# Exponents and phases of the S4D responses in two 64-row halves of the matmul array

## The chip, the cores and the metric

The kernel runs on one core of one Trainium2 chip. A core has a matrix engine (TensorE: PE for its matmuls, PEld for its weight loads), a vector engine (VectorE: DVE), an activation engine (ScalarE: ACT), a general engine (GpSimd: POOL) and a queue engine (SyncE: SP). They work side by side and wait for each other by semaphores. The metric is device time in microseconds; the time before is the median of three runs, 559.39 us (557.99 to 559.58).

## What is computed

Two branches over an input u of 2048 positions and 640 channels are mixed by a gate. The first is a convolution with a response K that is made from 128 states per channel; the second is a filter in the two-dimensional frequency plane.

```python
def _A_ref(u, log_A_real, A_imag, C_real, C_imag, log_dt, D_skip):
    dt = jnp.exp(log_dt)
    A = -jnp.exp(log_A_real) + 1j * A_imag
    C = (C_real + 1j * C_imag) * dt[:, None]
    P = jnp.exp((A * dt[:, None])[:, :, None] * pos[None, None, :])
    K = 2.0 * jnp.einsum("dn,dnl->dl", C, P).real          # 640 x 2048
    ...                                                    # y = causal convolution of u with K, by rfft / irfft
    return y + u * D_skip[None, None, :]

def _B_ref(x, w_r, w_i):
    return irfft2(rfft2(x) * (w_r + 1j * w_i))

g = sigmoid((x * gate_w).sum(-1, keepdims=True))
return g * _A_ref(...) + (1 - g) * _B_ref(...)
```

The change touches how K is made, nothing else.

## The kernel before

The body has three stages. In the first, `phase_p` prepares the parameters of the responses and `phase_a` begins the transform of u along the positions. In the second, two streams are merged: `ga` goes on with `phase_a` (the rest of the transform, the frequency filter and its way back; lines L372 to L640) and `phase_c` (the first transform of K), and `gl` runs `phase_b`, which makes K. In the third, `phase_d` multiplies the transforms of u and K, goes back and mixes.

`merge` issues the two streams in turn: each yields a weight for what it has issued, and the stream that has done the smaller share of its total (164.29 for `ga`, 76.8 for `gl`, the sum of its yields) goes next. The order so written is a priority; the tile framework's planner then fixes an order for each engine at compile time and may let later work pass earlier work that it expects to be waiting. On the chip each engine works through its own list in order.

`phase_b` works on 40 groups of 16 channels, with the 128 states on the partitions. A position is written as an outer step (64 j, 32 values) plus an inner one (64 values, symmetric about 31.5). For each group t:

- `mags(t)`: an exponent for 64 inner and 32 outer positions of 16 channels, 1536 columns. The rates lie in 96 rows (6 for each channel: three bf16 parts of the rate, three of the log magnitude of C), and a table `rm` that is zero outside each channel's own rows spreads them. Three matmuls (L700) of 96 rows and 512 columns go to one bank of PSUM each, and an Exp (L702) follows each. Five groups are done in a row, since Exp and Sin use different tables of ACT.
- `phases(t)`: outer phases (columns 512 to 1023) and inner phases (0 to 511) in revolutions. Each takes three accumulating matmuls (L710) over 128 rows: the phase plus a large constant, minus that constant (which rounds it), minus the phase. What is left is the negative of the fraction of a revolution.
- `trig(t)`: for the outer phases Abs (L723), Sin (L724) and a second Sin of the absolute value with a quarter turn as bias (the cosine, L725) on ACT, into `sc` in SBUF. For the inner phases the absolute value is taken on DVE (L720, a bitwise and), and ACT makes the sine `sx` (L726) and cosine `cx` (L727) into two PSUM banks of their own (pool `pt`, one buffer each).
- `prods(t)`: DVE multiplies the exponentials by sx (L734, L735) and cx (L736) to `x`; POOL multiplies the outer ones by sc (L739, L740) to `y`. It is issued after the phases and sines of group t+1.
- `kgen(t)`: 64 small matmuls of 32 weight columns (L753), four side by side in four column groups of the array, sum over the states; an ACT copy (L759) for each two groups and a store for each ten.

PSUM has 8 banks; in this stage `ga` has 3, the pool `ps` of p_e and p_p has 2 buffers of one bank, `pk` has 1 and `pt` has 2. The parameters of five groups come by two DMAs that POOL issues in `load` (L690).

The tile names in the profile are those of the code: p_e and p_p are the PSUM tiles of exponents and phases, e the exponentials, aq the absolute values. A tile written `128*64` is the part of the array that a matmul uses: rows by columns.

Of the kernel before, what the change touches and what calls it, by code (L numbers as in the profile page):

```python
# [9 lines left out]
F32 = mybir.dt.float32  # L10
BF = mybir.dt.bfloat16
I32 = mybir.dt.int32
# [8 lines left out]
N = 128  # L21
# [28 lines left out]
def _tables():  # L50
# [67 lines left out]


    j = np.arange(32)  # L120
    rp = np.zeros((4, 32, 2, 16, 32))
    rn = np.zeros((4, 32, 512))
    rn[0, 24] = -MAGIC
    one_row = np.zeros((8, 4, 8, 5, N))
    one_row[:, :, 0] = 1.0
    rm = np.zeros((16, 6, 16, 96))
    for x in range(16):
        g, i = x // 4, 6 * (x % 4)
        rp[g, i:i + 3, 0, x] = j + 0.5
        rp[g, i:i + 3, 1, x] = 64 * j  # L130
        rp[g, i + 3:i + 6, 1, x] = 1.0
        rm[x, 0:3, x, 0:64] = A_ORDER
        rm[x, 0:3, x, 64:96] = 64 * j
        rm[x, 3:6, x, 64:96] = 1.0
    rp, rn = rp.reshape(128, 1024), rn.reshape(128, 512)
    rq = rp.copy().reshape(4, 32, 2, 16, 32)
    for x in range(16):
        rq[(x // 4 + 2) % 4, 24, :, x] = MAGIC
    rp = np.concatenate([rq.reshape(128, 1024), -rp, rn], 1)
    f = lambda x: np.ascontiguousarray(x, dtype=np.float32)  # L140
    h = lambda x: np.ascontiguousarray(x, dtype=mybir.dt.np(BF))
    return {"t_c1": f(c1), "t_w2": f(w2), "t_w3": f(w3), "t_td": f(td),
            "t_rp": h(rp), "t_one": h(one_row), "t_rm": h(rm.reshape(96, 1536))}


def _lay_out(u, log_a, a_i, c_r, c_i, log_dt, d_skip, w_r, w_i, gate_w):
# [49 lines left out]
def body(tc, A, out):  # L196
    nc = tc.nc
    T = Ctx()
    with ExitStack() as top:
# [25 lines left out]
        with ExitStack() as cctx:  # L225
            def left():
                with ExitStack() as ctx:
                    T.bc = ctx.enter_context(tc.tile_pool(name="b_c", reuse_waits="tile", bufs=1))
                    T.rm = T.bc.tile([96, 1536], BF, name="rm")
                    T.rp = T.bc.tile([128, 2560], BF, name="rp")  # L230
                    yield from phase_p(tc, A, T)
                    yield from phase_b(tc, A, T, ctx)

            ga, gl = chain(phase_a(tc, A, T), phase_c(tc, A, T, cctx)), left()
            next(gl)
            next(ga)
            for n in (6, 15):
                next(gl)
                while len(T.cps) < n:
                    next(ga)  # L240
            next(gl)
            while T.pin is None:
                next(ga)
            merge((164.29, ga), (76.8, gl))
            phase_d(tc, A, T, cctx, out)


# [417 lines left out]
def phase_b(tc, A, T, ctx):  # L665
# [20 lines left out]

    def load(b0):
        for k in (1, 0):
            par = w2.tile([128 - 32 * k, BT, N], BF, tag="par%d" % k, name="par%d" % k)
            G.dma_start(par[:, :, :], par_v[k][b0 // BT])  # L690
            for t in range(b0, b0 + BT):
                pars[k][t] = par[:, t - b0, :]

    def mags(t):
        e = es[t] = ep.tile([128, 16, 96], F32, tag="e", name="e")
        ef = e.rearrange("p d i -> p (d i)")
        for c in range(0, 1536, 512):
            p = ps.tile([128, 512], F32, tag="ps", name="p_e")
            with after(T.pin):
                P.matmul(p[:, :], pars[1][t], rm[:, c:c + 512], start=True, stop=True)  # L700
            with after(st.trig):
                st.exp = S.activation(ef[:, c:c + 512], p[:, :], AF.Exp)  # L702
            yield 0.2

    def phases(t, r):
        r.p = {}
        for c in (512, 0):
            p = r.p[c] = ps.tile([128, 512], F32, tag="ps", name="p_p")
            for i, w in enumerate((rp[:, c:c + 512], rn, rq[:, c:c + 512])):
                P.matmul(p[:, :], pars[0][t], w, start=i == 0, stop=i == 2)  # L710
            yield 0.22

    def trig(t, r):

        aq = wt.tile([128, 2, 16, 32], F32, tag="w", name="aq")
        sc = r.sc = wt.tile([128, 2, 16, 32], F32, tag="w", name="sc")
        sx, cx = r.sx, r.cx = [pt.tile([128, 16, 32], F32, tag=n, name=n) for n in ("sx", "cx")]
        fl = lambda t: t.rearrange("p d i -> p (d i)")
        af = aq.rearrange("p v d i -> p (v d i)")
        V.tensor_scalar(out=af[:, 0:512].bitcast(I32), in0=r.p[0][:, :].bitcast(I32), scalar1=0x7FFFFFFF, scalar2=None, op0=ALU.bitwise_and)  # L720

        with after(st.exp):
            S.activation(af[:, 512:1024], r.p[512][:, :], AF.Abs)  # L723
        S.activation(fl(sc[:, 0]), r.p[512][:, :], AF.Sin, scale=TWO_PI)  # L724
        S.activation(fl(sc[:, 1]), af[:, 512:1024], AF.Sin, scale=-TWO_PI, bias=T.hpi)  # L725
        S.activation(fl(sx), r.p[0][:, :], AF.Sin, scale=TWO_PI)  # L726
        T.trig = st.trig = S.activation(fl(cx), af[:, 0:512], AF.Sin, scale=-TWO_PI, bias=T.hpi)  # L727

    def prods(t, r):
        e, sx, cx, sc = es[t], r.sx, r.cx, r.sc  # L730
# [32 lines left out]
    def run():  # L763
        pend = []
        load(0)
        yield 0.0
        for t in range(40):
            if t % BT == 0:
                if t:
                    prods(t - 1, rs[t - 1])  # L770
                    pend.append(t - 1)
                for x in range(t, t + BT):
                    yield from mags(x)
                    if len(pend) > 1:
# [12 lines left out]
        for x in (*pend, 39):  # L787
            yield from kgen(x)
# [268 lines left out]
```

## Time and profile before

| | |
|---|---|
| median of three runs | 559.39 us (557.99 to 559.58) |
| the profiled execution's own time | 560.56 us |
| its span, first to last instruction | 558.8 us |
| granted TensorE clock | 0.984 |
| PE / DVE / ACT / POOL busy, share of the span | 92% / 80% / 61% / 49% |

The profile has a page (busy times, slices, a chain of waits that ended last, the costliest groups of instructions) and views that can be asked: groups by line, one tile's instructions, waits, a timeline, and busy times in given windows. In a row of a group, the figures after the bar are the union of its busy time in us and the mean ns of one instruction, then the idle time of its engine just before them and who ended most of it. Matmuls are pipelined: the duration of one includes the way through the array, so that three in a row take much less than three times one. What a matmul costs in a stream is read from the starts in the timeline. Some matmul records are missing: 212 of the 240 phase matmuls are there.

### The profile page before, as it was taken

What the parts mean: (1) busy time and instruction counts of PE and PEld (TensorE: products, weight loads), DVE (VectorE), ACT (ScalarE), POOL (GpSimd) and SP (SyncE); (2) the same over time, 40 slices, a digit from 0 to 9 for tenths busy, and PEclk for the clock granted to TensorE, in tenths of its full rate; (3) what the DMA queues carried; (4) which work ended last, traced back from release to release, by engine and by line L of the source; (5) the groups of instructions that cost most, each with busy time, mean ns of one, the idle gap of its engine ahead of it and who ended that gap; (6) DMA issues with size and microseconds to landing.
All of it is one profiled execution on the core that took longest, in us unless ns stands there. A gap on an engine that the chain in (4) does not pass through costs nothing.

```text
span 558.8 us, 16697 instructions
## 1 busy us (share of the span) xinstructions
PE 516.2 (92%) x7124; PEld 394.9 (71%) x7152; DVE 447.5 (80%) x684; ACT 339.8 (61%) x626; POOL 273.9 (49%) x277
## 2 busy tenths in 40 slices
PE   8899899997989899998999989999799999999975
PEld 6789456665857576867777766767787887787741
DVE  5997279479799979999979979876296885977945
ACT  4674677585587689797899786898224223241210
POOL 4993254056246327346257546165163446648433
PEclk9999999999899999999999999999899999999979
DMA  8969233165250331353222132115958989899877
GB/s 322 373 203 347 95 111 110 21 234 187 64 197 17 129 123 60 81 166 128 79 60 71 49 81 95 54 49 190 390 210 267 347 285 354 281 294 316 259 237 265
DMA packets 47697, 100.61 MB, mean 180 GB/s; under 512 B 3492, under 2 KB 32952, under 8 KB 45960
## 3 DMA queue, kind: packets, MB, share of 16 engines
q1 hardware_dynamic: 25176, 67.41, 34.7%
q10 hardware_dynamic: 20080, 22.52, 12.4%
q0 software_dynamic: 2368, 9.64, 5.1%
q8 instruction: 56, 0.92, 0.7%
q14 instruction: 17, 0.14, 0.1%
HBM read 60.22 MB, written 39.65 MB: 179 GB/s over the span
## 4 chain that ended last, share of the span: by engine, by line
PE 37%; DVE 6%; DMA 3%; ACT 3%; issue 1%; ACTq 0%; DVEq 0%; POOL 0%; SPq 0%
PE p_s L372 6%; PE p_s L385 6%; PE p_i L893 5%; PE p_e L172 3%; PE p_p L710 2%; PE p_k L753 2%; PE p_c L972 2%; DMA s_d<-s 2%; PE p_e L700 2%; PE p_i L633 2%; PE p_t L557 2%; PE p_eo L618 2%; PE p_eo L619 1%; PE p_d L573 1%; PE p_d L574 1%
## 5 line engine op out<-in xcount | busy, mean ns | idle before, releaser
L385 PE MATMUL p_s<-t,w 128*64 128x160 f32 x1056 | 90.5, 308 | 4.7 <-ACT ut L420 2.3
L385 PEld LDWEIGHTS p_s<-t,w 128*64 128x64 f32 x1056 | 75.4, 136 | 15.3 <-issue 4.3
L739 POOL TENSOR_TENSOR y<-e,sc 128x512 f32<-128x512 f32 x40 | 53.5, 1339 | 57.3 <-ACT sc L724 42.6
L702 ACT ACTIVATE e<-p_e 128x512 f32<-128x512 f32 x120 | 69.2, 608 | 14.0 <-PE p_e L700 12.7
L710 PE MATMUL p_p<-rp,par 128*128 128x512 bf16 x212 | 63.0, 380 | 8.1 <-ACT sx L726 4.5
L373 ACT COPY t<-p_s 128x512 f32<-128x512 f32 x40 | 24.8, 623 | 63.6 <-PE p_s L372 46.8
L753 PEld LDWEIGHTS p_k<-x,y 128*32 128x32 f32 x2560 | 42.2, 109 | 25.1 <-issue 20.7
L753 PE MATMUL p_k<-x,y 128*32 128x64 f32 x2560 | 55.5, 222 | 0.9 <-DVE x L735 0.8
L740 POOL TENSOR_TENSOR y<-e,sc 128x512 f32<-128x512 f32 x40 | 53.7, 1342 | 0.0
L700 PE MATMUL p_e<-rm,par 96*128 96x512 bf16 x120 | 43.4, 383 | 7.6 <-ACT e L702 4.3
L862 DVE TENSOR_TENSOR ma<-p_s,us 128x640 f32<-128x640 f32 (+1 forms) x36 | 28.2, 783 | 27.7 <-issue 22.0
L736 DVE TENSOR_TENSOR x<-e,cx 128x1024 f32<-128x1024 f32 x40 | 48.4, 1209 | 0.0
L372 PEld LDWEIGHTS p_s<-c,kt 128*64 128x64 f32 x640 | 39.2, 139 | 12.6 <-issue 7.1
L372 PE MATMUL p_s<-c,kt 128*64 128x128 f32 x640 | 44.6, 278 | 3.4 <-issue 2.2
L893 PE MATMUL p_i<-t,w 128*64 128x160 f32 x528 | 43.6, 306 | 3.9 <-POOL t L868 3.6
L895 ACT COPY s<-p_i 128x640 f32<-128x640 f32 x32 | 21.7, 694 | 38.7 <-PE p_i L893 23.4
L868 POOL TENSOR_TENSOR t<-mb 64x320 f32<-64x320 f32 (+1 forms) x36 | 29.9, 832 | 30.5 <-DVE t L868 30.1
L893 PEld LDWEIGHTS p_i<-t,w 128*64 128x64 f32 x528 | 37.4, 139 | 8.8 <-POOL t L868 4.3
L868 POOL TENSOR_TENSOR t<-ma 64x320 f32<-64x320 f32 x32 | 28.3, 886 | 29.9 <-DVE ma L862 28.7
L372 PE MATMUL p_s<-c,u 128*64 128x128 f32 x640 | 40.3, 276 | 0.8 <-ACT ut L420 0.6
L372 PEld LDWEIGHTS p_s<-c,u 128*64 128x64 f32 x640 | 35.3, 136 | 7.4 <-issue 5.3
L710 PEld LDWEIGHTS <-par 128*128 128x128 bf16 x240 | 21.3, 97 | 25.9 <-issue 12.0
(164 smaller groups left out, 1172.6 us busy)
## 6 DMA issues: line engine op xcount, KB each, us to landing
u_d<-ut SPq DMA_DIRECT2D x32, 320.0 KB, 2.8
us<-u_d ACTq DMA_DIRECT2D x16, 640.0 KB, 6.2
s_d<-s ACTq DMA_DIRECT2D x15, 640.0 KB, 9.2
t<-s_d SPq DMA_DIRECT2D x14, 640.0 KB, 6.8
ww<-in_w_l SPq DMA_DIRECT2D x8, 642.0 KB, 5.1
ue<-u_d SPq DMA_DIRECT2D x8, 640.0 KB, 4.2
k_d<-kt SPq DMA_DIRECT2D x4, 1280.0 KB, 4.5
kt<-k_d SPq DMA_DIRECT2D x8, 640.0 KB, 5.6
```

What stands on the lines that cost most here:

```text
L372: nc.tensor.matmul(p[64 * ri:64 * ri + 64, j, :], src(i + j), e1[ri], start=True, stop=True)
L385: ins = nc.tensor.matmul(p[64 * j:64 * j + 64, i, 160 * ri:160 * ri + 160], w2[:, x, 64 * ri:64 * ri + 64], t1[:, x // 2 if x < 32 else K0 ...
L700: P.matmul(p[:, :], pars[1][t], rm[:, c:c + 512], start=True, stop=True)
L702: st.exp = S.activation(ef[:, c:c + 512], p[:, :], AF.Exp)
L710: P.matmul(p[:, :], pars[0][t], w, start=i == 0, stop=i == 2)
L736: V.tensor_tensor(out=x[:, 0].rearrange("p d (h j) -> p d h j", h=2), in0=e[:, :, 0:64].rearrange("p d (h j) -> p d h j", h=2), in1=cx.uns ...
L739: G.tensor_tensor(out=y[:, 1], in0=e[:, :, 64:96], in1=sc[:, 0], op=ALU.mult)
L740: G.tensor_tensor(out=y[:, 0], in0=e[:, :, 64:96], in1=sc[:, 1], op=ALU.mult)
L753: P.matmul(st.pb[32 * r:32 * r + 32, o, :], y[:, ri, 4 * qq + JR[r], :], x[:, ri, 4 * qq + JR[r], :], start=t % 2 + qq + 1 - ri == 0, stop ...
L862: V.tensor_tensor(out=ma[:nl, :hn], in0=pv, in1=uu, op=ALU.mult)
L868: return eng.tensor_tensor(out=t2[64 * im:64 * im + 64, o, :], in0=m[l, :hn, 0, :], in1=m[l, :hn, 1, :], op=ALU.add if im else ALU.subtract)
L893: T.mm = P.matmul(p[x:x + 64, i // 2, 160 * (i % 2):160 * (i % 2) + 160], T.w3[:, k0 + h + i, x:x + 64], t2[:, h + i, :], start=True, stop ...
```

## The change

The tables `rm` and `rp` are laid out in two halves of 64 rows, and 8 of the 16 channels of a group lie in each. The array is used as two parts of 64 rows and 128 columns, each with its own bank of PSUM: a matmul pair in place of one.

- Exponents: 1536 columns for 16 channels become 768 for 8 channels in each half, as a pair of 512 columns and a pair of 256 (48 rows of each half are used). The two Exps are over 1024 and 512 elements in place of three over 512. The parameter block of the exponents goes to partitions 0 to 47 and 64 to 111 by two DMAs in place of one.
- Outer phases: three accumulating pairs of 256 columns. Abs and both Sins read the two banks as one operand of 2 x 256.
- Inner phases: the cosine gets columns of its own, with a quarter of a revolution taken off in the table, so that half the columns give the sine and half the cosine. Three accumulating pairs of 512 columns; one Sin over 1024 elements, written back in place in PSUM. The bitwise and on DVE and the Sin with a bias go.
- The pool `ps` has two buffers of two banks in place of one bank; `pt` goes. `prods` reads the inner sines where the phases were, in a buffer of `ps`.
- `prods(t-1)` is now issued between the outer and the inner phases of t. The yields of `phase_b` change, and the total of `gl` with them (63.76).

```diff
-            merge((164.29, ga), (76.8, gl))
+            merge((164.29, ga), (63.76, gl))
...
-    wt = ctx.enter_context(tc.tile_pool(name="b_w", reuse_waits="tile", bufs=5))
+    wt = ctx.enter_context(tc.tile_pool(name="b_w", reuse_waits="tile", bufs=3))
+    wa = ctx.enter_context(tc.tile_pool(name="b_a", reuse_waits="tile", bufs=2))
...
-    pt = ctx.enter_context(tc.tile_pool(name="b_pt", reuse_waits="tile", bufs=1, space=PSUM))
...
-    rp, rq, rn = rp[:, 0:1024], rp[:, 1024:2048], rp[:, 2048:2560]
+    steps = rp[:, 0:768], rp[:, 768:1280], rp[:, 1280:2048]
...
         for k in (1, 0):
-            par = w2.tile([128 - 32 * k, BT, N], BF, tag="par%d" % k, name="par%d" % k)
-            G.dma_start(par[:, :, :], par_v[k][b0 // BT])
+            par = w2.tile([128, BT, N], BF, tag="par%d" % k, name="par%d" % k)
+            if k:
+                for j in range(2):
+                    G.dma_start(par[64 * j:64 * j + 48], par_v[1][b0 // BT, 48 * j:48 * j + 48])
+            else:
+                G.dma_start(par[:, :, :], par_v[0][b0 // BT])
...
     def mags(t):
-        ef = e.rearrange("p d i -> p (d i)")
-        for c in range(0, 1536, 512):
-            p = ps.tile([128, 512], F32, tag="ps", name="p_e")
+        ef = e.rearrange("p (j d) i -> p j (d i)", j=2)
+        for c, n in ((0, 512), (512, 256)):
+            p = ps.tile([128, 2, 512], F32, tag="ps", name="p_e")
             with after(T.pin):
-                P.matmul(p[:, :], pars[1][t], rm[:, c:c + 512], start=True, stop=True)
+                for j in range(2):
+                    x = slice(64 * j, 64 * j + 48)
+                    P.matmul(p[:, j, 0:n], pars[1][t][x], rm[x, c:c + n], start=True, stop=True)
             with after(st.trig):
-                st.exp = S.activation(ef[:, c:c + 512], p[:, :], AF.Exp)
-            yield 0.2
+                st.exp = S.activation(ef[:, :, c:c + n], p[:, :, 0:n], AF.Exp)
+            yield n * 0.0005
...
+    def phases(t, c, n):
+        p = ps.tile([128, 2, 512], F32, tag="ps", name="p_p")
+        for i, w in enumerate(steps):
+            y = 0 if i == 1 else c
+            for j in range(2):
+                x = slice(64 * j, 64 * j + 64)
+                P.matmul(p[:, j, 0:n], pars[0][t][x], w[x, y:y + n], start=i == 0, stop=i == 2)
+        return p
+
+    def outer(t, r):
+        p = phases(t, 512, 256)
+        aq = wa.tile([128, 2, 256], F32, tag="a", name="aq")
         sc = r.sc = wt.tile([128, 2, 16, 32], F32, tag="w", name="sc")
+        sv = sc.rearrange("p v (j d) i -> p v j (d i)", j=2)
         with after(st.exp):
+            S.activation(aq[:, :, :], p[:, :, 0:256], AF.Abs)
+        S.activation(sv[:, 0], p[:, :, 0:256], AF.Sin, scale=TWO_PI)
+        S.activation(sv[:, 1], aq[:, :, :], AF.Sin, scale=-TWO_PI, bias=T.hpi)
+
+    def inner(t, r):
+        p = phases(t, 0, 512)
+        f = p.rearrange("p j w -> p (j w)")
+        T.trig = st.trig = S.activation(f, f, AF.Sin, scale=TWO_PI)
+        r.sx, r.cx = f.rearrange("p (d v i) -> p v d i", v=2, i=32)[:, 0], f.rearrange("p (d v i) -> p v d i", v=2, i=32)[:, 1]
...
             rs[t] = Ctx()
-            yield from phases(t, rs[t])
-            trig(t, rs[t])
+            outer(t, rs[t])
+            yield 0.11
             if t % BT:
                 prods(t - 1, rs[t - 1])
                 pend.append(t - 1)
+            inner(t, rs[t])
+            yield 0.22
             if len(pend) > 2:
                 yield from kgen(pend.pop(0))
```

More of the change, by code (lines that the diff above doesn't have):

```diff
@@ L120, in _tables @@
     j = np.arange(32)
-    rp = np.zeros((4, 32, 2, 16, 32))
-    rn = np.zeros((4, 32, 512))
-    rn[0, 24] = -MAGIC
     one_row = np.zeros((8, 4, 8, 5, N))
     one_row[:, :, 0] = 1.0
-    rm = np.zeros((16, 6, 16, 96))
-    for x in range(16):
+    rm = np.zeros((2, 64, 8, 96))
+    rp = np.zeros((2, 32, 8, 96))
+    for x in range(8):
         g, i = x // 4, 6 * (x % 4)
[L129 to L139, printed above, removed]
+        rp[g, i:i + 3, x, 0:32] = rp[g, i:i + 3, x, 32:64] = j + 0.5
+        rp[g, i:i + 3, x, 64:96] = 64 * j
+        rp[g, i + 3:i + 6, x, 64:96] = 1.0
+        rp[g, 24, x, 32:64] = -0.25
+        rm[:, 6 * x:6 * x + 3, x, 0:64] = A_ORDER
+        rm[:, 6 * x:6 * x + 3, x, 64:96] = 64 * j
+        rm[:, 6 * x + 3:6 * x + 6, x, 64:96] = 1.0
+    rq = rp.copy()
+    for x in range(8):
+        rq[1 - x // 4, 24, x] = MAGIC
+    flat = lambda v: np.concatenate([v[..., 0:64].reshape(64, 512), v[..., 64:96].reshape(64, 256)], 1)
+    rn = np.zeros((64, 512))
+    rn[24] = -MAGIC
+    rp = np.tile(np.concatenate([flat(rq), rn, flat(-rp)], 1), (2, 1))
     f = lambda x: np.ascontiguousarray(x, dtype=np.float32)
@@ L228, in left @@
                     T.bc = ctx.enter_context(tc.tile_pool(name="b_c", reuse_waits="tile", bufs=1))
-                    T.rm = T.bc.tile([96, 1536], BF, name="rm")
-                    T.rp = T.bc.tile([128, 2560], BF, name="rp")
+                    T.rm = T.bc.tile([128, 768], BF, name="rm")
+                    T.rp = T.bc.tile([128, 2048], BF, name="rp")
                     yield from phase_p(tc, A, T)
@@ L701, in mags @@
             with after(st.trig):
-                st.exp = S.activation(ef[:, c:c + 512], p[:, :], AF.Exp)
-            yield 0.2
[L705 to L715, printed above, removed]
+                st.exp = S.activation(ef[:, :, c:c + n], p[:, :, 0:n], AF.Exp)
@@ L716, in trig @@
         sc = r.sc = wt.tile([128, 2, 16, 32], F32, tag="w", name="sc")
[L717 to L720, printed above, removed]
+        sv = sc.rearrange("p v (j d) i -> p v j (d i)", j=2)
         with after(st.exp):
-            S.activation(af[:, 512:1024], r.p[512][:, :], AF.Abs)
```

6 lines of the change are left out of this document (1 added, 5 removed).

## The prediction

> **What bounds the kernel now.** First the busy times of the three stages, to see where the change can act at all.
>
> ```profile
> core 0: us, PE busy (x) PEld busy (x) DVE busy (x) ACT busy (x) POOL busy (x), PEclk, DMA share, GB/s
> 0.00:66.00 66.00, 59.00 (x991) 50.64 (x991) 49.58 (x62) 39.46 (x76) 40.30 (x37) 1.00 0.79 280
> 66.00:396.00 330.00, 311.21 (x4402) 227.60 (x4427) 278.45 (x423) 258.75 (x484) 153.03 (x146) 0.99 0.32 107
> 396.00:558.80 162.80, 145.97 (x1736) 116.66 (x1735) 119.43 (x199) 41.63 (x68) 80.59 (x94) 0.96 0.84 289
> ```
>
> The merged stage is 330 us long, and PE (311), DVE (278) and ACT (259) are all near its length. POOL and the DMAs have room. Which of the three sets the pace is read from the chain that ended last, here between 272 and 376 us (it reaches no further back), with the pieces of one place in it.
>
> ```profile
> by line: PE p_p L710 12.3%; PE p_e L700 9.6%; PE p_i L633 9.4%; PE p_t L557 8.6%; PE p_eo L618 8.3%; PE p_k L753 8.0%; PE p_eo L619 7.6%; PE p_d L573 5.2%; PE p_d L574 4.9%; ACT cx L727 1.8%; ACT sc L725 1.8%; DVE mm L594 1.8%; DVE ff L606
> ...
> 331.34 0.60 DVE aq L720
> 331.94 0.61 DVE x L735
> 332.57 0.59 ACT sx L726
> 333.20 0.81 PE p_p L710 x3
> ...
> 342.44 0.69 DVE aq L720
> ```
>
> The nine PE entries make 73.9%: most of this chain is PE going from one matmul to the next. The two groups that the change rewrites, L710 and L700, are 21.9% of 104 us, 22.8 us. The first four pieces show the other kind of place: ACT's Sin waits until DVE has read the one buffer of sx, and PE waits for that Sin.
>
> **Matmul time.** What a matmul costs in a stream is read from starts.
>
> ```profile
> 208.14 0.44 PE L574 MATMUL p_d<-td,ft 65*128 65x160 f32 x2
> 208.41 0.44 PE L573 MATMUL p_d<-td,ft 128*128 128x161 f32 x2
> 208.69 0.81 PE L710 MATMUL p_p<-rp,par 128*128 128x512 bf16 x3
> 209.33 0.44 PE L574 MATMUL p_d<-td,ft 65*128 65x161 f32 x2
> ...
> 415.59 1.31 PE L893 MATMUL p_i<-t,w 128*64 128x160 f32 x16
> 416.67 0.77 PE L172 MATMUL p_e<-t3e,c 128*64 128x320 f32 x4
> ```
>
> Three phase matmuls take 209.33 - 208.69 = 0.64 us, 0.215 each. A group t has nine such matmuls (six L710, three L700): 1.935 us. No row shows two halves of rows side by side. The nearest is halves of columns: 16 matmuls of 64 columns in 416.67 - 415.59 = 1.08 us, 0.135 for a pair, as much as one of the full width (0.27 for the two of 208.14). If pairs of row halves do the same, a pair of 512 costs 0.215 and one of 256 half of it, 0.1075. After the change a group has four of 512 (one in the exponents, three inner) and four of 256: 1.29 us. That saves 0.645, times 40 25.8 us. The chain had 22.8 us of these lines where 104/330 of 40 groups, 12.6, cost 12.6 x 1.935 = 24.4: 93% is on the path. I take **-24.0**. With no overlap at all it is +24.0. I take the end with overlap, by the column rows, which are the nearest.
>
> The weight loads go from 9 to 16 a group. They stay hidden by the row of the column halves, where each recorded load is as long as the pair that covers it and two are needed.
>
> ```profile
> L385 PEld LDWEIGHTS p_s<-t,w 128*64 128x64 f32 x1056 | 75.4, 136 | 15.3 <-issue 4.3
> ```
>
> **Changing the shape of the array.** A matmul that uses another split of the array than the one before it starts late.
>
> ```profile
> 368.87 0.82 PE L710 MATMUL p_p<-rp,par 128*128 128x512 bf16 x3
> 369.62 0.46 PE L557 MATMUL p_t<-c,ff 64*128 64x64 f32 x4
> ...
> 360.35 0.38 PE L700 MATMUL p_e<-rm,par 96*128 96x512 bf16 x1
> 360.57 0.44 PE L618 MATMUL p_eo<-td,pmt 128*128 128x161 f32 x2
> ...
> L710 PE MATMUL p_p<-rp,par x212: 376/379/390, 70.6 to 381.4; 128*128 128x512 bf16 x106
> ...
> L700 PE MATMUL p_e<-rm,par x120: 376/379/634, 57.6 to 364.6; 96*128 96x512 bf16 x120
> ```
>
> From p_p in the full array to a tile of 64 rows it is 0.75 us for three, 0.10 over 0.645; from p_e (96 rows, the full array) to p_eo it is 0.22, nothing over 0.215. So today's exponents and phases slip between the full-width work of the other stream for free, and the 64-row pairs will pay on each side. I counted the neighbours in PE's timeline from the first of them to the last (57.6 to 381.4): the matmuls of the two lines lie in 171 unbroken runs, and 208 of their 342 sides, 61%, border on full-width work; the others border on p_k or other narrow tiles and pay already. After the change there are 160 tiles of pairs; with the 256-column exponents often next to another pair I take 130 runs: 260 x 0.61 x 0.10 = 15.9 us, 93% on the path, **+14.8**. Bounds: 80 new changes (runs twice as long) +8, all 320 sides +30.
>
> The Trainium skill has this as a rule against such a change: "Mode switching requires drain" (TensorEngine Tiling (Array Packing), Key Properties). The trace agrees, with 0.10 us at each change; by the rule alone no sum can be made.
>
> **DVE and ACT.** The rows of what goes and of what is merged:
>
> ```profile
> L702 ACT ACTIVATE e<-p_e 128x512 f32<-128x512 f32 x120 | 69.2, 608 | 14.0 <-PE p_e L700 12.7 <-POOL fg L541 0.2
> L895 ACT COPY s<-p_i 128x640 f32<-128x640 f32 x32 | 21.7, 694 | 38.7 <-PE p_i L893 23.4 <-DMA s_d<-s 9.3 <-DVE mb L863 5.5
> ...
> L634 ACT COPY s<-p_i 128x320 f32<-128x320 f32 x34 | 14.5, 441 | 4.4 <-PE p_i L633 4.4
> ...
> L726 ACT ACTIVATE sx<-p_p 128x512 f32<-128x512 f32 x40 | 23.9, 597 | 16.4 <-DVE x L735 15.6 <-DVE aq L720 0.5
> L727 ACT ACTIVATE cx<-aq,c 128x512 f32<-128x512 f32 x40 | 27.9, 698 | 1.8 <-DVE x L736 1.8
> L720 DVE TENSOR_SCALAR aq<-p_p 128x512 int32<-128x512 int32 x40 | 27.3, 683 | 8.2 <-PE p_p L710 7.6 <-issue 0.5
> ```
>
> DVE loses 40 x 683 ns = 27.3 us. On the chain of 104 us L720 has the two pieces quoted above, 1.29 together; times 330/104 = 3.17 that is **-4.1**. Bounds: 0, and -27.3 if DVE set the pace all the way. ACT: the copies of 640 and 320 elements give (694 - 441)/320 = 0.79 ns an element, so an instruction of 1024 costs 608 + 512 x 0.79 = 1012 as an Exp and 597 + 405 = 1002 as a Sin. Three Exps (1824) become 1620, and sx with cx (1295) becomes 1002: 0.50 us a group, 20 us of ACT's 259. On the chain stands cx with 1.8% of 104, 5.9 us over the stage; merging takes 293 of its 698 ns: **-2.5**, bounds 0 and -6 (cx gone).
>
> **The buffers.** In place of four banks there are two buffers of two. The inner sines stay where the phases were until `prods` has read them: one of two buffers is blocked through Sin (1.0 us) and three products on DVE.
>
> ```profile
> L736 DVE TENSOR_TENSOR x<-e,cx 128x1024 f32<-128x1024 f32 x40 | 48.4, 1209 | 0.0
> ...
> ACT sx L726 <- DVE x L735: 15.6, 10, 3.0
> ```
>
> Today DVE's delay stops ACT: ten times, 15.6 us, and 1.8 more before cx. Afterwards that wait falls to PE: the outer pair of t+2 needs the buffer that `prods(t)` frees, and behind it in PE's list stand the matmuls of the other stream, whose copies ACT and DVE then miss. It is also released later, by L736 and not by L735, 1.21 us. From below the cost is 0 (the planner lets other matmuls pass); from above all 17.4 us fall to PE and each of the ten gets 1.21 longer: +29.5. The one place where the chain shows this coupling is quoted above, and there it costs 1.21 more and saves the Sin's 0.59; at one in 104 us that is 0.62 x 3.17 = 2, and I take **+3.0**, near the lower end, since PE has other work ready through most of the stage.
>
> **What costs nothing.** POOL issues 8 more parameter DMAs:
>
> ```profile
> L690 POOL DMA_DIRECT2D par<-par_d x12 | 6.8, 570 | 31.7 <-PE p_g L459 16.6 <-PE p_e L700 9.8 <-PE p_p L710 3.8
> ```
>
> 8 x 0.57 = 4.6 us of a POOL that is busy 153 of 330; the products L739 wait behind them, and if they were late each time it would be 4.6. The bytes are the same. The smaller tables load before 57.6, when nothing waits for them. Three buffers for sc and two for aq replace five shared ones, and each user waits for what it waited for. The new weights of `merge` move the streams against each other with the same end; bounds unknown in sign, a few us either way in the range.
>
> **Sum.** -24.0 + 14.8 - 4.1 - 2.5 + 3.0 = -12.8 us. The span goes from 558.8 to 546.0, the profiled execution's own 560.56 to 547.8; the median of the runs lies 1.17 below that execution, so **546.6**. Its own range is 540 to 553.
>
> **Rivals.**
> - *Slower: PE takes over ACT's wait.* The buffer mechanism at its upper end, +29.5 in place of +3.0: 573.1. It decides from the point where the wait costs more than 15.8 us. For it: ACT's 17.4 us of waits, and DVE at 278 of 330. Against: in the 104 us of chain the coupling shows once.
> - *The pairs don't overlap, or only in part.* With none, +24.0 in place of -24.0: 594.6. With half, 570.6. For it: no row shows row halves together. Against: column halves do.
> - *No gain: PE loses on changes of shape what it saves.* All 320 sides at 0.10, +30 in place of +14.8: 561.8. Or a pair costs 1.3 of one matmul, a third of the way to no overlap: 1.29 x 1.3 = 1.68 a group, 0.258 saved, 9.6 us on the path in place of 24.0: 561.0. For it: 0.10 stands in the rows; against the second, the column halves.
> - *DVE sets more of the pace.* If the bitwise and counts for 12 us and not 4.1, as it would where DVE is busiest, 538.7. For it: DVE's 278 us; against, the chain.
>
> The Trainium skill gives a speedup of 3.07 for four row tiles side by side (TensorE: Matmul & The Clock Gate, Measured speedup vs the span model), not 4; a pair that lost the same share would cost 1.30 of one matmul, the second form of the last-but-one rival. No run here shows row tiles yet.
>
> **How the numbers follow.** Forecast 0.46; DVE sets more 0.14; no gain 0.14; PE's wait 0.17; little or no overlap 0.09. A measurement of this kernel tells 0.3%, 1.7 us, from no change. Faster by more: 0.46 + 0.14 + 0.02 of the no-gain case = 0.62; within: 0.10 of it; slower: 0.02 + 0.17 + 0.09 = 0.28. The range from 533 to 574 takes in all but the worst overlap and the tails.
>
> **What would show it.** The two matmuls of a pair of p_p start a few ns apart, and the next pair 0.215 us later: the overlap. 0.10 us at each side of a run: the changes of shape. No bitwise and, and DVE near 251 us in the stage; ACT near 239. Idle time of PE before p_p that ends with DVE's x L736: the buffers. The forecast is wrong if PE waits there for more than 15 us, or if pairs start 0.2 us apart.

## The result, and the profile after

The changed kernel took 585.23 us, the median of four runs (583.25 to 587.75); the kernel before took 559.49 beside it. The ratio is 1.046, 95% interval 1.040 to 1.051: slower by 26 us, where 13 us faster had been forecast. Here and below, medians and ratios leave out the slow runs, those more than 1.5% above the fastest of the same kernel. The profiled execution took 584.63 us, its span is 582.8, the granted clock 0.968 (before 0.984).

The busy times of the three stages, with the columns of the first fence of the prediction:

```profile
0.00:66.00 66.00, 59.65 (x1002) 51.76 (x1002) 49.43 (x62) 39.77 (x73) 41.38 (x39) 0.97 0.76 276
66.00:420.00 354.00, 316.91 (x4692) 226.50 (x4686) 266.35 (x383) 248.98 (x406) 147.10 (x152) 0.96 0.31 100
420.00:583.00 163.00, 145.23 (x1750) 116.36 (x1746) 118.39 (x199) 42.29 (x68) 80.77 (x94) 0.98 0.84 286
```

All of the loss lies in the merged stage: 354 us for 330, the others as before. In it PE is busy for 316.9 us (311.2 before) and idle for 37.1 (18.8 before), and its clock is 0.96 for 0.99. So of 24.0 us, 18.3 are new idle time of PE and 5.7 more busy time, although it streams less. DVE (278.5 to 266.4) and ACT (258.8 to 249.0) have less to do, and still the stage is longer.

First the two things that were meant. PE's timeline of the changed kernel (start, duration to the modelled end, engine, line, operation, tiles, count):

```profile
207.88 0.50 PE L718 MATMUL p_p<-rp,par 64*128 64x256 bf16 x6
208.31 0.54 PE L575 MATMUL p_d<-td,ft 65*128 65x161 f32 x2
...
209.78 0.44 PE L574 MATMUL p_d<-td,ft 128*128 128x161 f32 x2
210.15 0.82 PE L718 MATMUL p_p<-rp,par 64*128 64x512 bf16 x6
210.91 0.54 PE L575 MATMUL p_d<-td,ft 65*128 65x161 f32 x2
211.28 0.44 PE L574 MATMUL p_d<-td,ft 128*128 128x160 f32 x2
211.56 0.43 PE L575 MATMUL p_d<-td,ft 65*128 65x160 f32 x2
```

Six phase matmuls of 64 rows and 512 columns hold PE for 210.91 - 210.15 = 0.76 us: three times 0.215, plus 0.10 for the change of shape behind them. Before, three full ones took 0.64. So the two halves of a pair run side by side, fully. Six of 256 columns take 0.43, which is half of 0.64 plus 0.10. And the two f32 matmuls ahead of a run take 0.37 where two take 0.27 in a stream: 0.10 on that side as well. There is a third 0.10, which neither the forecast nor its count of sides has: the two f32 matmuls behind the run take 211.28 - 210.91 = 0.37 too, and only the next two the usual 211.56 - 211.28 = 0.28.

Next what PE waited for in the merged stage, from the view of waits of each kernel (who <- for whom: us in total, times, longest). Before:

```profile
PE p_p L710 <- ACT sx L726: 4.5, 5, 1.4
PE p_e L700 <- ACT e L702: 4.3, 5, 1.4
PE p_p L710 <- ACT sc L724: 2.1, 4, 1.1
```

After:

```profile
PE p_e L707 <- DVE x L744: 11.1, 4, 4.4
PE p_p L718 <- ACT sc L728: 6.4, 16, 0.7
PE p_i L634 <- DVE xx L584: 4.4, 2, 2.3
PE p_s L386 <- DVE ut L421: 4.0, 2, 3.0
PE p_s L373 <- POOL kt L823: 3.2, 1, 3.2
PE p_p L718 <- DVE x L744: 2.0, 6, 0.6
```

L744 is the last of the products of `prods` (L736 before): it lets go of the two banks in which the inner sines lie. PE waits 13.1 us for it, most of it not before the phases but before the *exponents*, and four times only; the longest is 4.4. The waits behind it (xx, ut, kt) belong to the other stream; that they follow from its late turn is not shown.

The longest of these waits, on DVE and PE:

```profile
175.30 0.82 DVE L599 TENSOR_TENSOR pm<-zz 128x642 f32<-128x642 f32 x1
176.04 0.82 DVE L600 TENSOR_TENSOR pm<-zz 128x642 f32<-128x642 f32 x1
176.78 0.68 DVE L743 TENSOR_TENSOR x<-e,p_p 128x512 f32<-128x512 f32 x1
177.38 1.65 DVE L606 TENSOR_TENSOR ff<-pm 128x640 f32<-128x640 f32 x1
178.95 1.88 DVE L607 TENSOR_TENSOR ff<-pm 128x640 f32<-128x640 f32 x1
180.75 1.21 DVE L744 TENSOR_TENSOR x<-e,p_p 128x1024 f32<-128x1024 f32 x1
...
177.21 0.44 PE L575 MATMUL p_d<-td,ft 65*128 65x161 f32 x2
182.01 0.61 PE L707 MATMUL p_e<-rm,par 48*128 48x512 bf16 x2 [4.37 <-DVE x L744]
182.55 0.90 PE L574 MATMUL p_d<-td,ft 128*128 128x160 f32 x2
183.25 0.74 PE L575 MATMUL p_d<-td,ft 65*128 65x160 f32 x2
```

And the busy times in this place, with the columns of the first fence:

```profile
172.00:177.00 5.00, 4.62 (x71) 3.63 (x66) 5.00 (x10) 3.02 (x6) 0.68 (x2) 1.00 0.79 239
177.00:182.00 5.00, 0.64 (x5) 0.49 (x4) 5.00 (x5) 1.71 (x2) 4.68 (x5) 0.77 0.16 60
179.00:180.00 1.00, 0.00 (x0) 0.00 (x0) 1.00 (x2) 0.00 (x0) 1.00 (x1) 0.87 0.06 10
182.00:184.00 2.00, 1.99 (x10) 1.22 (x13) 2.00 (x5) 1.02 (x1) 0.00 (x0) 0.50 0.00 0
184.00:188.00 4.00, 4.00 (x66) 3.46 (x67) 1.97 (x4) 0.60 (x1) 1.06 (x2) 0.68 0.00 0
186.00:186.50 0.50, 0.50 (x3) 0.50 (x3) 0.00 (x0) 0.00 (x0) 0.44 (x2) 0.50 0.00 0
186.50:187.00 0.50, 0.50 (x4) 0.39 (x3) 0.00 (x0) 0.00 (x0) 0.20 (x1) 0.93 0.00 0
```

DVE is never idle here. Between two products of the same group stand two operations of the filter, L606 and L607, and they take 1.65 and 1.88 us, twice their usual 0.82 (as pm has it), while POOL is busy for 4.68 of these 5 us. PE's list has the exponents next, they need the banks that L744 reads, and the ready matmuls of p_d stand behind them. The price isn't over when the wait is: the granted clock is 0.50 in the next two us and 0.68 in the four after that, and two f32 matmuls behind a run take 183.25 - 182.55 = 0.70 us for the 0.37 above. The Trainium skill says that the array's clock falls to half after an idle window of about 3.4 us (TensorE: Matmul & The Clock Gate, Part 1). The rows agree on the half, but not on the time: PE's last matmul ended at 177.65 (a modelled end), and the clock fell between 179 and 180 (0.87 in that us, 0.50 later), after some 2 us. By 187 it was full again (0.50 from 186.0 to 186.5, 0.93 from 186.5 to 187.0).

### The profile page after: what moved, and what is told of

Read it like the earlier page. It is cut to its first block, busy times and chain, and to the rows that moved or that the text cites. A ratio compares the mean times of both kernels' runs of the same rounds, so it can differ in the third digit from the quotient of the medians.

```text
span 582.8 us, 17178 instructions
## 1 busy us (share of the span) xinstructions
PE 521.8 (90%) x7432; PEld 394.6 (68%) x7432; DVE 434.2 (74%) x644; ACT 331.0 (57%) x546; POOL 269.2 (46%) x285
## 3 DMA queue, kind: packets, MB, share of 16 engines
q10 hardware_dynamic: 20080, 22.52, 11.9%
## 5 line engine op out<-in xcount | busy, mean ns | idle before, releaser
L709 ACT ACTIVATE e<-p_e 128x1024 f32<-128x1024 f32 x80 | 62.5, 812 | 32.3 <-PE p_e L707 28.7
L747 POOL TENSOR_TENSOR y<-e,sc 128x512 f32<-128x512 f32 x40 | 52.1, 1303 | 39.7 <-ACT sc L728 22.9
L718 PE MATMUL p_p<-rp,par 64*128 64x256 bf16 (+1 forms) x480 | 52.8, 327 | 9.7 <-ACT sc L728 6.4
L761 PEld LDWEIGHTS p_k<-x,y 128*32 128x32 f32 x2560 | 44.2, 115 | 20.5 <-issue 19.3
L761 PE MATMUL p_k<-x,y 128*32 128x64 f32 x2560 | 56.8, 229 | 0.1
L744 DVE TENSOR_TENSOR x<-e,p_p 128x1024 f32<-128x1024 f32 x40 | 48.5, 1212 | 0.0
L734 ACT ACTIVATE p_p<-p_p 128x1024 f32<-128x1024 f32 x40 | 41.0, 1024 | 9.2 <-ACT sc L729 4.9
L707 PE MATMUL p_e<-rm,par 48*128 48x512 bf16 (+1 forms) x160 | 30.5, 346 | 14.6 <-DVE x L744 11.1
L742 DVE SCALAR_TENSOR_TENSOR x<-e,p_p 128x512 f32<-128x512 f32 x40 | 27.2, 681 | 21.5 <-ACT p_p L734 19.9
```

Source lines behind the costliest of these rows:

```text
L707: P.matmul(p[:, j, 0:n], pars[1][t][x], rm[x, c:c + n], start=True, stop=True)
L709: st.exp = S.activation(ef[:, :, c:c + n], p[:, :, 0:n], AF.Exp)
L718: P.matmul(p[:, j, 0:n], pars[0][t][x], w[x, y:y + n], start=i == 0, stop=i == 2)
L734: T.trig = st.trig = S.activation(f, f, AF.Sin, scale=TWO_PI)
L744: V.tensor_tensor(out=x[:, 0].rearrange("p d (h j) -> p d h j", h=2), in0=e[:, :, 0:64].rearrange("p d (h j) -> p d h j", h=2), in1=cx.uns ...
L747: G.tensor_tensor(out=y[:, 1], in0=e[:, :, 64:96], in1=sc[:, 0], op=ALU.mult)
```

## The experiments

At the start three theories were open. **A**: the loss is that of banks held until DVE has done its products. **B**: it lies in PE's own work or in the order in which the two streams are issued. **C**: it is POOL's parameter loads. Each comparison below is with the kernel before, run on the same chip.

**e1, the sines to SBUF.** The changed kernel, with the inner Sin written to SBUF, so that ACT frees the banks.

```diff
-        f = p.rearrange("p j w -> p (j w)")
-        T.trig = st.trig = S.activation(f, f, AF.Sin, scale=TWO_PI)
+        f = wa.tile([128, 1024], F32, tag="s", name="sx")
+        T.trig = st.trig = S.activation(f[:, :], p.rearrange("p j w -> p (j w)"), AF.Sin, scale=TWO_PI)
```

> The changed kernel, with one edit: the inner Sin writes to a tile in SBUF (two buffers) and not in place in PSUM, so that a buffer of phases comes free when ACT has read it and not when DVE has made its products. Theory A (PE waits for the buffer that DVE's products hold): PE's idle time before the exponents and phases that ends with DVE's x L744 (11.1 us in 4 waits and 2.0 us in 6) is gone, the low clock behind the long waits with it, and the time falls from 585 to 560-570 us. Rival B (the changes of shape of the array alone make it slow): it stays at 580-588. Rival C (POOL's parameter loads, late): it stays too.

Measured: 617.24 us, ratio 1.101 (1.096 to 1.106). PE no longer waits for L744, as A wants, but the kernel is slower still, where 560 to 570 had been expected. The products of the changed kernel, and then those of e1, in their groups:

```profile
L744 DVE TENSOR_TENSOR x<-e,p_p 128x1024 f32<-128x1024 f32 x40 | 48.5, 1212 | 0.0
L742 DVE SCALAR_TENSOR_TENSOR x<-e,p_p 128x512 f32<-128x512 f32 x40 | 27.2, 681 | 21.5 <-ACT p_p L734 19.9 <-PE p_k L761 1.7
L747 POOL TENSOR_TENSOR y<-e,sc 128x512 f32<-128x512 f32 x40 | 52.1, 1303 | 39.7 <-ACT sc L728 22.9 <-PE p_k L761 11.3 <-ACT p_p L734 5.0
```

```profile
L744 DVE TENSOR_TENSOR x<-e,sx 128x1024 f32<-128x1024 f32 x40 | 59.3, 1482 | 0.0
L742 DVE SCALAR_TENSOR_TENSOR x<-e,sx 128x512 f32<-128x512 f32 x40 | 47.6, 1190 | 18.5 <-ACT sx L734 12.0 <-PE p_k L761 6.4
L747 POOL TENSOR_TENSOR y<-e,sc 128x512 f32<-128x512 f32 x40 | 69.4, 1735 | 49.0 <-PE p_k L761 29.8 <-ACT sc L728 18.7 <-ACT sc L729 0.3
```

With both operands in SBUF a product takes 1190 ns where it took 681 with one in PSUM, and POOL's products beside it take 1735 for 1303. The edit took away one wait and brought another cost, so it doesn't judge A. It suggests a reason for the slow filter operations above: they too have both operands in SBUF. The Trainium skill has this as a rule, that a DVE instruction with two SBUF inputs contends with a GpSimd instruction that reads SBUF (SBUF — State Buffer, Who interferes with whom). The rows agree.

**e2, e3, e4: order of the streams, neighbours of the pairs, loads.** e2 gives `merge` and the yields of `gl` the old shares; e3 yields once, after both pairs of exponents, so that they stand together; e4 lets SP issue the parameter loads (shown for one of the two tiles; the yields of e2 are not shown).

```diff
-            merge((164.29, ga), (63.76, gl))
+            merge((164.29, ga), (76.8, gl))
...
-            yield n * 0.0005
+        yield 0.384
...
-                G.dma_start(par[:, :, :], par_v[0][b0 // BT])
+                nc.sync.dma_start(par[:, :, :], par_v[0][b0 // BT])
```

> The changed kernel, with the yields of the response stream scaled so that the shares of exponents (0.6 a group), phases (0.44) and sums (0.88) and their total (76.8) are those of the kernel before. If the altered interleaving of the two streams made it slow, 565 or less; Theory A and Rival B: the buffers and the shapes are the same, so 580-590.

> The changed kernel, with one yield after both pairs of exponents of a group (0.384) in place of one behind each, so that the two pairs stand together more often. By the price of 0.10 us for each change of shape and up to 2 fewer for each of 40 groups: 0 to 8 us less, 577-585. Theory A: the waits for the buffers stay, so not below 575. Rival B: the same 577-585, and the count of changes falls with it.

> The changed kernel, with the parameter blocks loaded by SP and not by POOL, where POOL stands idle 44 us before the issue (for PE's last exponents of the block before) and 16 us (for its phases) with the products y behind it. Rival C: POOL's products come earlier and the time falls by 5 us or more, below 580. Theory A and Rival B: 582-588.

Measured: e2 584.28 us (ratio 1.036 to 1.049), e3 582.42 (1.033 to 1.043), e4 592.24 (1.052 to 1.066). The shares of the two streams aren't it. Nor are POOL's loads: with SP issuing them the kernel doesn't get faster (why it gets slower is not known). In e3 the changes of shape counted in the records of the merged stage fall from 379 to 351; 28 at 0.096 us (a finer estimate of the 0.10 above) are 2.7, and the kernel gained 2.8. The intervals of the two kernels overlap, so this isn't shown; it only has the size that the price of a change gives.

**e5, the kernel before with its sine in place.** Hold a bank for DVE, leave everything else. The freed bank of sx goes to `ps`, which then has three.

```diff
-    ps = ctx.enter_context(tc.tile_pool(name="b_ps", reuse_waits="tile", bufs=2, space=PSUM))
+    ps = ctx.enter_context(tc.tile_pool(name="b_ps", reuse_waits="tile", bufs=3, space=PSUM))
...
-        sx, cx = r.sx, r.cx = [pt.tile([128, 16, 32], F32, tag=n, name=n) for n in ("sx", "cx")]
+        sx, cx = r.sx, r.cx = r.p[0].rearrange("p (d i) -> p d i", i=32), pt.tile([128, 16, 32], F32, tag="cx", name="cx")
```

> The kernel before, with one part of the change alone: the inner sine is written in place over the inner phases and stays in that buffer of ps until DVE's products have read it. ps gets the bank that sx had (3 buffers of one bank in place of 2), the cosine keeps its own. Full-width matmuls as before, so no added change of shape. Theory A (a buffer of phases held by DVE's products is what costs): PE waits for DVE's x before its exponents and phases, and the time is 565 or more. If holding a buffer is harmless by itself: 557-562, or less, as ACT no longer waits for the buffer of sx (15.6 us).

Measured: 557.1 us, ratio 0.993 (0.989 to 0.998): not slower, a little faster. Holding a bank for DVE isn't a cost by itself where two others are left; A as it stood has fallen.

**e7a and e7b, less DVE.** From the kernel before (a) and the changed one (b), the four DVE operations of the filter that make pm and ff, and POOL's copy between them, are left out (32 us of DVE in the kernel before, 36 in the changed one). If a late DVE is what the changed kernel suffers from, it gains more.

```diff
-            pm = tile5("pm", E + 1)
-            V.tensor_tensor(out=pm[:nl, 0:2, :E], in0=zz[:nl, 0:2], in1=zz[:nl, 2:4], op=ALU.add)
...
-            V.tensor_tensor(out=half(ff, 161, 80), in0=lo, in1=hi, op=ALU.subtract)
+            st.pm = zz
```

> The kernel before without the four DVE operations and one POOL copy that follow the filter in each of 9 blocks (pm and ff: sums and differences and their fold; zz is used in their place, the matmuls stay the same), about 31 us less on DVE. It is the reference for the next run: 535-555.

> The changed kernel without the same operations (pm and ff). They stand in front of DVE's products in the waits of 4 us before the exponents. Theory A: with them gone the buffers come free earlier, and the changed kernel is at most 12 us over the kernel before without them (25 us with them). Rival B (changes of shape, PE alone): the distance stays at 22-28 us.

Measured: a 561.28 us (0.9995 to 1.006), b 578.36 (1.027 to 1.037). The kernel before gains nothing from 32 us less of DVE: these operations don't set its pace. The changed one gains 7. The distance falls from 26 to 17, between the two expectations. That points to a late DVE as a part of the loss.

**e8, products at once.** The changed kernel issues `prods(t)` right behind `inner(t)`, not after the outer phases of t+1.

```diff
...
-            if t % BT:
-                prods(t - 1, rs[t - 1])
-                pend.append(t - 1)
             inner(t, rs[t])
+            prods(t, rs[t])
+            pend.append(t)
             yield 0.22
...
```

> The changed kernel, with the products of group t issued right behind its inner Sin and not after the outer phases of t+1. Their rank in DVE's list rises, so the buffer comes free earlier. Theory A: PE's waits for x L744 (13 us) shrink to less than half, 570-580. Rival B: 583-588.

Measured: 573.7 us, ratio 1.026 (1.021 to 1.031), 11.5 us less. Its waits of PE:

```profile
PE p_p L718 <- DVE x L744: 9.0, 7, 2.3
PE p_e L707 <- DVE x L744: 8.8, 4, 3.3
```

The time fell, but not by the way that was meant: PE waits more for L744 than in the changed kernel, 17.8 us for 13.1. What went are waits of the other stream (xx 4.4 us, gone; ut 4.0, now 0.8). Putting the products earlier in the text doesn't put the buffer out of PE's way.

**e9a and e9b, without POOL's y.** The changed kernel (a), and e1 (b), without the two products y of each group; y is one tile, set once, so that the k matmuls work on constant data.

```diff
-        y = wk.tile([128, 2, 16, 32], F32, tag="y", name="y")
+        if t == 0:
+            st.y = w1.tile([128, 2, 16, 32], F32, tag="y", name="y")
+            G.memset(st.y[:, :, :, :], 0.0)
+        y = st.y
...
-        G.tensor_tensor(out=y[:, 1], in0=e[:, :, 64:96], in1=sc[:, 0], op=ALU.mult)
-        G.tensor_tensor(out=y[:, 0], in0=e[:, :, 64:96], in1=sc[:, 1], op=ALU.mult)
```

> The changed kernel without POOL's products y (both operations of each group left out; the sums read a constant tile), so that POOL reads SBUF beside DVE only in the other stream. It is the reference for the next run: 575-585, as POOL was not on the path.

> The same without POOL's products, and with the inner Sin written to SBUF, so that the buffer of phases is free when ACT has read it. If the loss of the run with the Sin in SBUF (617 us) was that DVE and POOL slow each other when both read two operands from SBUF, DVE's x products are near 680 and 1210 ns again here. Theory A (the held buffer costs PE's waits): at least 10 us below the run without y and with the sines in place. If the hold is harmless: the same within 5 us.

Measured: a 557.54 us, ratio 0.997 (0.994 to 0.999), 28 us less than the changed kernel, where 575 to 585 had been expected, although PE's matmuls are the same; b 562.11 (1.002 to 1.007). That the k matmuls no longer wait for y can't be the reason: in the changed kernel their weight loads wait for it twice, 0.4 us in all. A filter operation in the changed kernel, then in e9a:

```profile
L527 DVE TENSOR_TENSOR fo<-ue 128x640 f32<-128x640 f32 (+1 forms) x9 | 12.5, 1393 | 0.0
```

```profile
L527 DVE TENSOR_TENSOR fo<-ue 128x640 f32<-128x640 f32 (+1 forms) x9 | 8.0, 888 | 0.0
...
L745 DVE SCALAR_TENSOR_TENSOR x<-e,p_p 128x512 f32<-128x512 f32 x40 | 27.3, 682 | 23.1 <-ACT p_p L734 22.9 <-PE p_k L762 0.3
```

The filter operations with two SBUF operands come down (this one from 1393 to 888 ns), and in e9b the product from SBUF that took 1190 ns takes 720. So most of e1's loss was the contention of DVE and POOL. With y gone, PE's waits for the last product fall to 4.3 us (2.3 and 2.0), and freeing the banks (b) gains nothing over holding them (a).

**e11, two buffers for three.** A new theory, **D**: it isn't the hold, but one of only two buffers being held. e5 with two one-bank buffers is the kernel before with one line changed, and has no row halves.

```diff
-        sx, cx = r.sx, r.cx = [pt.tile([128, 16, 32], F32, tag=n, name=n) for n in ("sx", "cx")]
+        sx, cx = r.sx, r.cx = r.p[0].rearrange("p (d i) -> p d i", i=32), pt.tile([128, 16, 32], F32, tag="cx", name="cx")
```

> The kernel before with the inner sine in place (the run of 557.7 us), with two buffers of phases and exponents in place of three; full-width matmuls. Theory D (it costs when one of only two buffers is held by DVE's products): PE waits for DVE's x before exponents and phases come back, 10 us or more in all, and the time is 570 or more. If the loss needs the row halves: 557-563.

Measured: 583.11 us, ratio 1.043 (1.039 to 1.047). A loss as large as that of the change, at full width. The merged stage of e5, and then of e11 with its first waits:

```profile
66.00:388.00 322.00, 304.18 (x4383) 225.93 (x4409) 275.25 (x423) 255.88 (x481) 152.49 (x146) 0.99 0.33 109
```

```profile
66.00:418.00 352.00, 323.60 (x4400) 234.49 (x4443) 292.82 (x423) 261.52 (x486) 148.93 (x146) 0.96 0.31 103
```

```profile
PE p_p L710 <- DVE x L735: 6.8, 8, 1.8
PE p_e L700 <- DVE x L735: 5.1, 3, 2.4
```

The same signs as in the changed kernel: PE waits for DVE's x, 11.9 us (2.5 in e5), its idle time grows by 10.6 us (352 - 323.6 against 322 - 304.2), and its clock goes from 0.99 to 0.96. The rest of the 30 us is PE's busy time, 19.4 us more for the same matmuls. About 10 of these are the clock, an estimate from 0.03 of 324. Some 5 more are changes of shape, 56 at 0.096: PE's order changed with the edit, and its timeline counts 255 of them for 199 in e5. The rest is open.

**e12, three buffers and products at once.** e5 with the order of e8.

> The kernel before with the inner sine in place in three buffers, and the products of a group issued right behind its sines. If the early products took 10 us off the changed kernel by the order on DVE alone, they take some off here too: 548-556. If they helped there by the buffer only: 555-560.

Measured: 551.81 us, ratio 0.987 (0.985 to 0.988). It beats both kernels, the one before by 1.3%, with full-width matmuls.

**e9c and e11b: what y costs where nothing is short, and where it is.** Both without y, by the edit of e9a: the kernel before, and e11.

> The kernel before without POOL's two y products per group (y is a constant tile, so the k matmuls use constant data). The changed kernel without them took 557.5 us, 28 us less than with them. If the loss comes from buffers held until a late VectorE has done its products, the kernel before, which holds none, gains little from a faster VectorE: 552 to 560 us, and the changed kernel is then within 6 us of it. If the y products slow both kernels alike (by reading SBUF beside VectorE), the kernel before falls as far: 525 to 540 us, and the distance of 25 us stays.

> The kernel before with the inner sine written in place and two one-bank buffers (583.1 us with the y products), here without the y products (constant y tile). Held buffers theory: the filter operations fall from about 1.4 to 0.9 us, VectorE's products come earlier, the buffer is free earlier, and most of the 25 us go: 555 to 568 us. Rival, that two buffers with one held cost what they cost however early VectorE is: 575 to 585 us.

Measured: e9c 556.31 us (0.990 to 0.995), e11b 558.56 (0.993 to 0.999). The kernel before loses only 4.5 us by y, the changed one 28, e11 24.5. So two buffers with one held cost 23.3 us with y (e11 less the kernel before, 559.82 beside it) and 2.3 without (e11b less e9c). Neither the short buffers nor the slow DVE costs much alone; together they cost over 20. The merged stage of e9a, and then of e9c:

```profile
66.00:394.00 328.00, 307.42 (x4710) 219.57 (x4704) 243.69 (x384) 249.57 (x405) 41.84 (x72) 0.99 0.33 108
```

```profile
66.00:388.00 322.00, 311.00 (x4434) 226.97 (x4433) 269.66 (x423) 258.27 (x484) 45.80 (x66) 0.99 0.33 110
```

At the same clock the row halves take 311.0 - 307.4 = 3.6 us off PE's busy time, far less than the streams alone would.

**e13, row halves where buffers aren't as short.** e12 with the exponents alone in row halves, each half into a one-bank buffer of its own.

```diff
-        for c in range(0, 1536, 512):
-            p = ps.tile([128, 512], F32, tag="ps", name="p_e")
...
-                P.matmul(p[:, :], pars[1][t], rm[:, c:c + 512], start=True, stop=True)
...
+        for c, n in ((0, 512), (512, 256)):
+            p = [ps.tile([128, 512], F32, tag="ps", name="p_e") for j in range(2)]
...
+                    P.matmul(p[j][:, 0:n], pars[1][t][x], rm[x, c:c + n], start=True, stop=True)
```

> The fastest kernel so far (before, inner sine in place, three one-bank buffers, products at once: 551.8 us) with the exponents alone in two 64-row halves, each half into a one-bank buffer of its own, phases at full width. TensorE: 40 x (3 - 1.5) x 0.215 = 12.9 us fewer streams, some 80 more changes of array shape at 0.096 = 7.7 us back; ACT: four exponentials per group for three, 40 x 0.2 = 8 us more, off the chain in most places. If row halves pay as the streams say and three buffers are enough: 545 to 551 us. If two buffers taken at once out of three make TensorE wait for ACT and for VectorE's products again: 556 to 575 us.

Measured: 573.6 us, ratio 1.024 (1.018 to 1.030), from two runs, 571.7 and 575.5. The profiled execution took 581.77 us; only the order of its matmuls is read from it:

```profile
139.01 0.28 PE L707 MATMUL p_e<-rm,par 48*128 48x256 bf16 x1
139.22 0.49 PE L386 MATMUL p_s<-t,w 128*64 128x160 f32 x2
139.65 0.63 PE L761 MATMUL p_k<-x,y 128*32 128x64 f32 x26
140.21 0.28 PE L707 MATMUL p_e<-rm,par 48*128 48x256 bf16 x1
```

The two halves stand 1.2 us apart, with other matmuls between them. Since each waits for a buffer of its own, the order of PE's list has torn many of the pairs: 49 of the 80 pairs of exponents have other matmuls between them, and the stage has 356 changes of shape for 193 in e12 (163 at 0.096 are 15.6 us). Torn pairs don't overlap, so this run says nothing on what row halves bring where buffers suffice. It suggests that a pair should share one buffer.

## Why the prediction was wrong

**What bounds the kernel**: PE, as the forecast has it. e7a agrees.

**Overlap of the pairs**: right. In the rows a pair of 512 columns costs what one full matmul did, 0.215, so the streams of the 40 groups fall by 25.8 us, as forecast.

**Changes of shape, +14.8**: the count was right, the price too low. There are 379 in PE's timeline for 232, and at 0.096 us each that is 14.1 us more, for 15.9 on PE in the forecast. The rule that the prediction quotes from the Trainium skill held. But where a full-array f32 matmul comes first behind a change, it takes another 0.10, as after 210.91 above. PE's timeline has 116 such places for 32, and 84 at 0.10 are 8.4 us. Together 22.5, so streams and changes leave a gain of 3.3 us, where 0.096 alone would give 11.7. The 3.6 of e9a and e9c agrees. With 9.5 for the clock (below), PE's busy time should grow by 6.2 us, and it grew by 5.7.

**DVE, -4.1, and ACT, -2.5**: nothing of either is seen. The bitwise and went (27.3 us), but the stage's DVE time fell by 12.1 only, to 266 and not 251: the four operations that make fo and ff cost 44.5 us for 32.0, now that POOL's y overlaps them more. e7a, where 32 us less of DVE brought nothing, suggests 0, though for other operations. ACT's instructions cost what was worked out (two Exps at 812 ns a group, 1624 for 1620; the Sin 1024 ns for 1002); no run isolates what that was worth.

**The buffers, +3.0**: this is the step that failed, and it carries most of the miss. The mechanism was named, with its place and even with "behind it in PE's list stand the matmuls of the other stream"; the size was taken near the lower end, "since PE has other work ready through most of the stage". PE has the work ready, but not in reach: its list is in order, and the ready matmuls stood behind the one that waited. What it measured, with DVE and ACT at nothing: 24.0 us of stage and the 3.3 that streams and changes gave, some 27 by subtraction. New idle time (18.3) and the clock's 9.5 come to as much. Of the miss of 36.8 us (24.0 for -12.8), that is 24; the changes of shape are 8 and DVE and ACT 7, and the streams gave 2 more back.

The upper end of 29.5 comes near, but in part by luck, since three things were missing from it. It counted waits of ACT that would move to PE, all at the phases; 11.1 of the 13.1 us stand at the exponents, which shared the two buffers of `ps` before too, when ACT freed them and not DVE. It left DVE's products at their own duration; in DVE's list they stand behind filter operations that took up to twice as long beside POOL. And it had no clock: the granted clock fell from 0.99 to 0.96 over the stage, about 9.5 us by an estimate from 0.03 of the 317 us.

The sign that was to show the forecast wrong, more than 15 us of PE waiting for x before p_p, was set on the wrong tile and too simply: 2.0 us there, 13.1 with p_e. The total of idle time, +18.3, showed it better than any one wait.

The chain of the kernel before was read rightly, but it can't hold a wait that isn't there yet. One piece in 104 us was scaled to the stage, as if the frequency of a coupling stayed the same when the banks of the sines went and two buffers were left for everyone.

**What costs nothing**: the weights of `merge`, right (e2). Moving POOL's loads away brought nothing (e4).

**The rival "PE takes over ACT's wait"** was the right one, at 573.1; with 22.5 for the changes of shape, 25.8 for the streams and nothing from DVE and ACT its sum comes to about 586, for 585.2 measured. What stays open is how the loss divides between the held buffer itself, the other stream's late turn and the clock behind each wait: they come together in every run. Open in part is why even without y the changed kernel isn't ahead (557.5 against 556.3): PE has 3.6 us less to do, but in the traces shown it is idle for 20.6 us against 11.0 (e9a's is of its longest run, 563.0). It waits 6.3 us for sc (2.1 in e9c) and 4.3 for x there, which points to the two buffers again; the 8 banks hold no third buffer of two, so no run shows row halves with one.

## What to carry to other kernels

Before packing two results into one buffer, count how many buffers remain for everybody who uses the pool, and who frees each. Holding one of three for a busy engine cost nothing here, holding one of two cost 26 us more (e11 less e5), and most of the price in waits of the changed kernel fell on a tile that hadn't waited for that engine directly. An engine that works through its list in order has "other work ready" only if that work stands ahead of the wait; and on PE a wait of a few us can be paid twice, once idle and once at a lower clock.

## What the hardware showed

DVE and POOL slow each other when both read two SBUF operands: 681 to 1190 ns on DVE, 1303 to 1735 on POOL (e1), and DVE is back at 720 when POOL's products are gone (e9b). A product with one operand in PSUM took 681 ns beside POOL and 682 without it. To leave an operand in PSUM was worth more here than the bank it held (585 us, 617 in e1).

A change between row halves and the full array cost about 0.10 us on the matmul ahead of it, and 0.10 more on a full-array f32 matmul that came first behind it (0.37 for 0.27 us of two, on both sides of a run).

In a wait of 4.4 us the granted clock fell to 0.50 some 2 us after PE's last matmul (0.87 in the us from 179 to 180, 0.50 later), and it came back only 4 to 5 us after the work began at 182.01 (0.50 from 186.0 to 186.5, 0.93 from 186.5 to 187.0).
